# A new written order for all parts of a one-core block kernel, with G and M2 laid in turn over two PSUM tiles

## The chip, the cores and the metric

The kernel runs on one core of one Trainium2 chip. Its time is device microseconds of one execution. The kernel before took 641.51 us (median of 3 runs, 640.56 to 641.72).

## The reference

One block of 2048 rows (S) and 512 columns (D): a linear attention with 32 heads and then a gated MLP that mixes the rows, each behind a layer norm whose scale, shift and gate come from a vector `c`. Cut to what matters:

```python
mod = (_silu(c) @ w_mod).reshape(c.shape[0], 6, 1, -1)
sa, ca, ga, sb, cb, gb = ...
h = _layernorm(x) * (1 + ca) + sa
x = x + ga * A(h)        # q, k, v = h @ wqkv; phi(t) = where(t > 0, t + 1, exp(t)) + 1e-6
                         # kv = sum_s phi(k) v;  z = sum_s phi(k);  o = phi(q) kv / (phi(q) z + 1e-6);  o @ wo
h = _layernorm(x) * (1 + cb) + sb
x = x + gb * B(h)        # z = gelu(h @ w_in), 1376 wide; z1, z2 = halves; z2 = layernorm(z2)
                         # g = w_sp @ z2 + b_sp, w_sp is 2048 x 2048;  (z1 * g) @ w_out
```

## The kernel before

All operands are fp32. A product is made of three matmuls (`mm3`): each operand is split into a hi part (fp32r, by ScalarE) and a lo part (what is left, a subtraction), and hi x hi, hi x lo and lo x hi are summed in PSUM. So nearly every tile passes ScalarE (hi) and VectorE or GpSimd (lo) on its way to TensorE. The rows are 16 tiles of 128.

Nothing is scheduled by a planner at run time or build time: `ORDER`, a string of 1954 words, says in which order the parts are emitted, and each engine (PE, ACT, DVE, POOL) and SP, which issues all 270 transfers, takes its own instructions in that order. A word is a two-letter part and its numbers; a part with a `yield` goes on at the word's next appearance. An instruction waits until what it reads is written and until the buffer that it writes is free. `SLOTS` says which buffer of a pool each new tile gets (`st`, four raw halves and transposing buffers; `s4`, split operands; `tq`, four late tiles; `ps...`, PSUM).

The stages and the words that matter here:

- Start: `lx` loads a tile of x, `s1` its statistics, `xm` subtracts the mean, `bh`/`bl` are its hi and lo parts, `ta th tl` turn it on PE and split it. `lm` loads w_mod, `mv` sums it on DVE, `cr ce` make a column of it on PE and ACT, `qh qd` split the weights of k and q with it. `du` are two dummy products each while the first loads come in.
- Attention: `km`, `qm` project a tile to k and q (12 matmuls each); `kr`, `ka` or `k1`, `k2`, `k4` are phi, `kh kl` its split; `gm` adds a tile to G (h transposed times phi(k), four blocks of 128 rows in two PSUM tiles). `gh` splits a block of G, `kv` multiplies by the weights of v, `kx` adds, masks and splits the result, `mm` makes a block of M2 (kv times w_o), `me` takes it out of PSUM. `d1 d2` are the denominators. `wo` is phi(q) times M2, `x1` the residual and its statistics.
- A tile is turned either on PE (`at`/`ht`, taken out by `ae`/`he`) or by a transposing DMA of its two 16-bit planes: `ap`/`hp` make the planes on ACT and issue the DMA (second appearance), `am`/`hm` merge the planes again, `ah al`/`hh hl` split. `Up Ux Ug` do this for the last stage.
- Gelu products: `z0`, `z1` (`za zb` in halves), `g1 g2` the gelu, `zl zn` the second layer norm. Their weights are loaded raw (`lW`), split (`wh wl`), stored (`ws`) and fetched back whole (`wr`).
- The product with w_sp takes seven products in place of eight per pair of row tiles (sums of halves beforehand, `Ss` for w_sp and `Td` for z2, and after it `Cs`). `Lh` loads half a row tile of w_sp, `Fh`/`Fl` split, `Pr` multiplies (12 matmuls of 344 columns).
- Output: `Um` multiplies by z1 (`Lz`), the result is turned (`Up Ux Ug`), for 14 tiles stored and fetched again (`Us Ul`), split (`Uh Uo`), multiplied by w_out (`Om`, 17 matmuls; weights by `Wl Wm Wh Wo`) and added to the residual (`Lx`, `Ot`, which then stores).

A trailing number of `am hm Ug` names the engine of the merge (0 DVE, 1 POOL, 2 ACT), and likewise the last number of `Fl`, `bl`, `Tb`, `Wo` and others, where a default stands without it.

Of the kernel before, what the change touches and what calls it, by code (L numbers as in the profile page):

```python
# [25 lines left out]
ta:0123453041025430154023525021301253213402141501305  # L26
psb:01010101101011010101011010101010101010
zs:0123456789abcdef2346ed32c5ea1d0e62c31e421c5e0243ea543c5e434c052ec520187b9fe6da4031c25978ec019b5a89367e124fdc0b8af
pst:0101111010101100100001010101001
s4:01234567307152364712156370453126507635670653105063573264507175723601450120736124325730460367412071530642352105462407316524136570241530652061543704327614657134021736574120176341564761354760253017251634106172171204156320  # L30
tb:01234567012401573450352327132302346202715362751261520350642431567155043617556405610701032327302174272651700417627436724163750134154
st:01230132122102120213131321032310321013012130102130101320302101230213321023103210
ws:010110
pso:0101010011010101101010101011010101010100010101010
md:0123102310210212021201
z1:01101010110110111
tq:01233220231203210010123013
u:0101100101101001
# [4 lines left out]
def block_kernel(ctx: ExitStack, tc: tile.TileContext, x, w_qkv, w_o, w_in, w_sp, b_sp, w_out,  # L43
# [48 lines left out]
    def mm3(o, a_hi, a_lo, b_hi, b_lo, first, last, skip=False):  # L92
        kw = {"skip_group_check": True} if skip else {}
        mm(o, a_hi, b_hi, start=first, stop=False, **kw)  # L94
        mm(o, a_hi, b_lo, start=False, stop=False, **kw)  # L95
        mm(o, a_lo, b_hi, start=False, stop=last, **kw)  # L96
# [900 lines left out]
    def cut():  # L997
# [19 lines left out]
        bh0 kr0 lx6 bl3,1 tl1 ba1 lx9 s16 s11 xm6 bb1 be1 s16 qd0,3 vp0 km1 lx5 s15 xm5 ka2,1 k22 ka0 k20 k20 km4 bl1
        kr1 qd0,2 bp2 qd0,0 k40 kh0 bl0 k14 ks0 ta5 th5 lW1,0 k22 ta6 ka1 k21 s15 tl5 qm3 ba2,0 ba3,0 bh5 k42 lw2,1 bx0
        bx0 th6 vh2 kl0 bl5,1 k21 k24 km5 k15 k41 gm0 lx7 vh0 bb0 s19 qm2 vp1 wh1,0 va1 xm9 tl6 s17 ks1,0 be0 q13 kh1
        s17 kl1 lx10 lW0,1 k24 km6 wl1,0,0 xm7 kh2 k44 kh4 kl2 ks2,0 ka3,1 k23 k23 gm1 k16 ta7 wh0,1 wl0,1 k43 vl0 vl2  # L1020
        ks3,0 k25 q12 bh4 ta9 th9 bl4 bh6 bl6 qm1 kh3 kl3 gm2 gm3 lx8 lW1,2 kl4 ws1,0 k25 k45 ws0,1 bh9 ks4,0 lx12 lW0,3
        vp2 lx11 wh0,3 ks5,0 qr1 tl9 s112 th7 wl0,3 km9 bh7 va2 s18 vh1 xm8 s19 lW1,3 tl7 s110 k19 gm4 wh1,2 wl1,2,0
        ws0,3 q23 k26 q23 q43 k26 kh5 vl1 wh1,3 lW1,1 bh8 kl5 k29 bl7 k46 ta8 km7 k17 wl1,3,0 k29 lW0,2 s111 k49 th8
        xm12 qm0 ws1,2 bl9 wh1,1 xm10 ta12 th12 tl12 s18 wl1,1,0 kh6 qm6 lM2 ta10 gm5 mV2,0 lx14 q22 qr0 xm11 q22 kl6
        q42 bl8,1 tl8 k27 k27 vp3 k47 va3 s110 ks6 ws1,1 th10 q16 s114 qa0,1 wh0,2 lW0,0 km12 tl10 wl0,2,0 q26 q26 ws1,3
        km8 kh7 k18 cv kl7 lx13 s113 s112 k112 k212 ta11 th11 gm6 gm7 q46 wh0,0 k28 wl0,0,0 lo1 mV2,1 k28 k48 ks7 ks8,0
        ks9 vh3 vl3 qm5 q15 mS2 mS2 tl11 ws0,2 s114 lo0 s111 kh9 kl9 kh8 km10 k110 lx15 s115 km11 xm14 kl8 bh14 k210 qa1
        k212 k412 mB2 qm4 xm15 gm8 gm9 k210 k410 mB2 wg1 bh15 s113 xm13 q20 q20 ta13 k111 k211 k211 lM4 bl14,1 bh10
        mV4,0 mV4,1 kh10 bl10 ks10,0 lM3 kl10 q14 k411 th13 tl13 kh11 cv q24 q24 bl15 gm10 kl11 q25 ks11,0 q25 q44 q45
        bh11 bl11 ks12 km13 ta14 th14 bh12 s115 lX4 k113 tl14 mk qm7 q17 q40 ta15 k213 k213 k413 th15 tl15 km14 wg0,1  # L1030
        k114 k214 k214 q27 ws0,0 kh12 mV3,0 mV3,1 k414 q27 ks13,0 kh13 kl13 gm11 mS3 kh14 kl12 kl14 km15 k115 k215
        ks14,0 qm8 q18 wg3,1 k215 k415 ks15,0 bl12,1 gm12 lX7 q47 mS3 kh15 kl15 zx qm10 q21 q21 mS4 wg2 bh13 wx3 wr0,0
        zx mS4 zs zr mB4 mB4 lX3 wx1 bl13,1 d10 q110 q210 d16,0 d26 d26 wr0,3 q210 d26 d26 mB3 q41 d20 q410 qm12 qm13
        d20 ap6 mB3 d20 d20 d14,0 q112 q212 q28 q113 q28 ap6 d24 q212 wx0 d110,0 vb gm13 q213 gm14 d24 d24 q213 q413
        q412 gm15 gh0 gh0 gh3 gh3 d17 d13,0 gh1 gh1 d27 gh2 gh2 d27 qm11 q111 d24 d113,0 am6,2 ap4 ap4 wy1 d27 d27 lX0
# [6 lines left out]
        wr1,2 ah10 Nb al10,0 hp4 x12 x11 x17 z00 x12 h22 ah13 al13 lX10 hp4 g10 wo10 zb0 d28 wo5 d28 x17 hp6 hm4 q414  # L1042
        lX5 hh4 hl4 x11 h21 x110 q411 hp2 hp2 hm3 g20 d111,0 d211 hh3 zl0 d28 x15 hp6 hm6,0 hl3,1 z04 g14 hh6 d19 d29
        hl6 z13 lX12 ht1 x17 x15 z16 x15 x15 d29 d29 hm2,0 g23 hh2 h25 d211 d211 d211 hp5 hp5 g26 x110 zl3 d29 ap8 ap12
        x110 zl6 h27 hl2,1 ap8 am8,2 zl6 zn6 zn6 q415 d115 z03 ap12 x110 h210 ah8 z14 g24 lX9 lX13 g14 hp7 wo13 g13
        mV5,0 am12 ah12 al12 x113 d215 ap9 d215 zl4 hp7 hm7,0 hm5,0 hh5 hl5 hh7 hl7 d215 z02 g12 d215 zl0 zn0 zn0 z12
        ap9 am9 z17 g22 lX8 hp10 hp10 x113 wo12 lX15 x113 ap15 d114,0 zl2 ah9 al9,0 zl3 zn3 d214 d214 al8,0 ap11 ap11
        Ta0,1 x112 x112 zl4 zn3 wo9 g12 z15 zn4 x19 hm10,0 g27 zl7 Tb0,1 wo8 d214 x113 h213 hp13 hp13 lX11 am11 z05 ah11
        x18 g25 zl2 al11,0 wo11 z06 he1 zn2 zl5 zl5 hh10 zn5 x19 zn2 Ta1,1 x112 hl10 zl7 x18 d214 x19 Ta1,0 x112 he1 g15
        ap15 x18 h212 am15,2 ah15 al15 Tb1,1,1 ap14 Td1,0,1 g16 ap14 am14 x18 h28 hp12 g13 ah14 al14,0 wo15 hp12 z11 zn4  # L1050
        g21 x19 g16 h29 Td1,1,1 Ta1,2 hp9 hp9 zl1 x111 x111 x111 x111 zl1 mV5,1 zn5 Ta2,0 x115 zn1 Tb1,2 hp8 hm9,0 z010
# [95 lines left out]
```

## Time and profile before

| | |
|---|---|
| runs | 641.51 us median, 640.56 to 641.72 |
| profiled execution | 642.65 us, span of the instructions 640.8 us |
| PE busy | 619.1 us, 3447 matmuls |
| DVE, ACT, POOL busy | 462.6, 368.6, 248.7 us |
| DMA | 99.99 MB, queue 1 53.2% of 16 engines |

The span runs from the first to the last instruction; the time has some 2 us around it. A busy PE is not PE at its peak, as matmuls overlap. PE is the engine in use nearly throughout, so idle stretches of PE are what another order can change; an engine's waits are read from the list of who waited for whom, and the work around them from the timeline.

### The profile page before, as it was taken

What the parts mean: (1) busy time and instruction counts of PE and PEld (TensorE: products, weight loads), DVE (VectorE), ACT (ScalarE), POOL (GpSimd) and SP (SyncE); (2) the same over time, 40 slices, a digit from 0 to 9 for tenths busy, and PEclk for the clock granted to TensorE, in tenths of its full rate; (3) what the DMA queues carried; (4) which work ended last, traced back from release to release, by engine and by line L of the source; (5) the groups of instructions that cost most, each with busy time, mean ns of one, the idle gap of its engine ahead of it and who ended that gap; (6) DMA issues with size and microseconds to landing.
All of it is one profiled execution on the core that took longest, in us unless ns stands there. A gap on an engine that the chain in (4) does not pass through costs nothing. (4 is left out here: it accounts for less than half of the span.)

```text
span 640.8 us, 9574 instructions
## 1 busy us (share of the span) xinstructions
PE 619.1 (97%) x3447; PEld 563.7 (88%) x3447; DVE 462.6 (72%) x806; ACT 368.6 (58%) x639; POOL 248.7 (39%) x218
## 2 busy tenths in 40 slices
...
GB/s 312 141 106 165 211 261 164 67 113 27 149 274 219 68 146 131 129 134 97 180 56 86 145 96 209 137 163 189 86 161 188 175 100 226 213 251 175 149 167 178
DMA packets 86287, 99.99 MB, mean 156 GB/s; under 512 B 56448, under 2 KB 56960, under 8 KB 86240
## 3 DMA queue, kind: packets, MB, share of 16 engines
q1 hardware_dynamic: 86240, 99.38, 53.2%
q8 instruction: 27, 0.44, 0.3%
...
## 5 line engine op out<-in xcount | busy, mean ns | idle before, releaser
L882 PE MATMUL P<-f,f 128*128 128x344 f32 x960 | 169.5, 321 | 3.5 <-POOL f L868 2.1
L882 PEld LDWEIGHTS P<-f,f 128*128 128x128 f32 x960 | 154.1, 188 | 5.9 <-POOL f L868 3.0
L649 PE MATMUL z<-win,ht 128*128 128x344 f32 x768 | 125.9, 323 | 4.8 <-ACT ht L111 2.5
L649 PEld LDWEIGHTS z<-win,ht 128*128 128x128 f32 x768 | 122.6, 190 | 8.4 <-ACT ht L111 2.9
L865 ACT ACTIVATE f<-raw_wsp 128x512 fp32r<-128x512 f32 x96 | 57.5, 624 | 59.8 <-DMA raw_wsp<-in_w_sp 19.8
L868 POOL TENSOR_TENSOR f<-raw_wsp,f 128x512 fp32r<-128x512 f32 x34 | 48.1, 1426 | 81.2 <-ACT f L865 57.1
L868 DVE TENSOR_TENSOR f<-raw_wsp,f 128x512 fp32r<-128x512 f32 x62 | 50.4, 830 | 27.0 <-ACT f L865 26.9
L220 POOL TENSOR_TENSOR mv<-ve,mhalf 128x1 f32<-128x1 f32 x48 | 34.8, 745 | 46.2 <-DVE ve L218 41.9
L882 PE MATMUL P<-bigb,f 128*128 128x344 f32 x192 | 39.9, 321 | 1.9 <-DVE f L868 1.9
L882 PE MATMUL P<-biga,f 128*128 128x344 f32 x192 | 39.4, 320 | 0.0
L94 PE MATMUL pout<-wo,ut 128*128 128x512 f32 (+1 forms) x85 | 32.7, 384 | 2.0 <-ACT ut L941 2.0
L96 PE MATMUL pout<-wo,ut 128*128 128x512 f32 (+1 forms) x85 | 32.7, 385 | 1.7 <-DVE ut L948 1.7
L882 PEld LDWEIGHTS P<-bigb,f 128*128 128x128 f32 x192 | 32.0, 188 | 2.5 <-DVE f L868 2.5
L95 PE MATMUL pout<-wo,ut 128*128 128x512 f32 (+1 forms) x85 | 32.3, 380 | 0.0
L882 PEld LDWEIGHTS P<-biga,f 128*128 128x128 f32 x192 | 32.1, 188 | 0.0
L232 ACT COPY ux<-us 128x768 uint16<-128x768 uint16 x32 | 25.0, 829 | 4.8 <-PE P L882 2.2
L588 POOL TENSOR_TENSOR pq<-pq,den 128x512 f32<-128x512 f32 x16 | 17.5, 1097 | 21.6 <-DVE den L585 20.3
L94 PE MATMUL qp<-wq,ht 128*128 128x512 f32 x64 | 25.8, 403 | 0.0
L94 PE MATMUL g<-pkhl,hhl 128*128 128x512 f32 x64 | 25.4, 397 | 0.0
L94 PE MATMUL po<-m,pt 128*128 128x512 f32 x64 | 25.4, 396 | 0.0
L94 PE MATMUL kp<-wk,ht 128*128 128x512 f32 x64 | 25.3, 396 | 0.0
L96 PE MATMUL po<-m,pt 128*128 128x512 f32 x64 | 25.3, 395 | 0.0
(234 smaller groups left out, 1391.5 us busy)
## 6 DMA issues: line engine op xcount, KB each, us to landing
raw_wsp<-in_w_sp SPq DMA_DIRECT2D x32, 512.0 KB, 4.7
raw_mod<-in_w_mod SPq DMA_DIRECT2D x12, 512.0 KB, 5.4
...
```

The costliest lines, as they stand in the source:

```text
L94: mm(o, a_hi, b_hi, start=first, stop=False, **kw)
L95: mm(o, a_hi, b_lo, start=False, stop=False, **kw)
L96: mm(o, a_lo, b_hi, start=False, stop=last, **kw)
L220: nc.gpsimd.tensor_tensor(mv[:, 1:2], ve, mhalf, op=OP.pow)
L232: nc.scalar.copy(pl[:, h], v[:, :, h])
L588: nc.gpsimd.tensor_mul(q3, q3, d[:, :, None].to_broadcast([P, H, D // H]))
L649: mm(p[:, b, :HB], a[:, i, kc], win[h][:, j, kc, b * HB:(b + 1) * HB], start=kc == 0 and k == 0, stop=kc == KC - 1 and k == 2)
L865: nc.scalar.activation(SF[p, h, k][:, 0], s_src(p, h, k), AF.Copy)
L868: eng.tensor_sub(SF[p, h, k][:, 1], s_src(p, h, k), f(SF[p, h, k][:, 0]))
L882: mm(B[p, k][:, :HB], a[:, x_], b[:, y_], start=i == 1, stop=i == 3 * NP)
```

## The change

`ORDER` and `SLOTS` are replaced as a whole: the same 1954 words in another order, except that some words name another engine. Counted from the words: DVE 806 to 784 instructions, ACT 637 to 647, POOL 211 to 223 (without set-up and table loads); PE's 3447 matmuls and SP's transfers are the same ones. Four functions lay the four blocks of G and of M2 over their two PSUM tiles in turn (0 and 2, 1 and 3) and no longer in pairs (0 and 1, 2 and 3).

```diff
-            mm3(G[dc // 2][:, dc % 2, :], a[:, 0, sl], a[:, 1, sl], b[:, 0], b[:, 1], t == 0, t == NT - 1)
+            mm3(G[dc % 2][:, dc // 2, :], a[:, 0, sl], a[:, 1, sl], b[:, 0], b[:, 1], t == 0, t == NT - 1)
...
     def m2_mm(g):
-        if g // 2 not in PM2:
-            PM2[g // 2] = ps("b", [P, 2, D], f"pm2_{g}")
-        mm3(PM2[g // 2][:, g % 2, :], KV["h"][:, 0, g], KV["h"][:, 1, g], wog[g][:, 0], wog[g][:, 1], True, True)
+        if g % 2 not in PM2:
+            PM2[g % 2] = ps("b", [P, 2, D], f"pm2_{g}")
+        mm3(PM2[g % 2][:, g // 2, :], KV["h"][:, 0, g], KV["h"][:, 1, g], wog[g][:, 0], wog[g][:, 1], True, True)
...
-        yield from hi_lo(o[:, 0], o[:, 1], PM2[g // 2][:, g % 2, :])
+        yield from hi_lo(o[:, 0], o[:, 1], PM2[g % 2][:, g // 2, :])
...
-        yield from hi_lo(GH[dc][:, 0], GH[dc][:, 1], G[dc // 2][:, dc % 2, :])
+        yield from hi_lo(GH[dc][:, 0], GH[dc][:, 1], G[dc % 2][:, dc // 2, :])
```

Of the order, the stretches that the prediction speaks of. The start:

```diff
-        lx3 s13 lx0 si si du1 du2 du3 du4 du5 du6 du7 du8 du9 du10 s10 xm3 lx4 s14 li lx2 s12 bh3 du11 lx1 s13 du12 ta3
-        th3 tl3 du13 du14 du15 du16 xm2 bh2 ta2 du17 s11 th2 du18 du19 du20 du21 du22 xm1 s14 xm4 lm1,0 mv1,0 s10 ta4
-        lm1,1 tl2 lm0,0 mv1,1 mv1,2 mv1,3 bh1 cr1 ce1 s12 mv0,0 du23 du24 du25 du26 du27 xm0 lm0,1 mv0,1 lw1,0 mv0,2
-        mv0,3 qh1,1 qd1,1 qh1,0 qd1,0 cr0 ce0 lw1,1 ta0 qh1,2 bl2 th0 qh1,3 qd1,2 qd1,3 km3 by0 km2 lw0,0 tl0 bp0 qh0,1
...
+        lx3 du1 s13 li du2 du3 du4 lx0 si si du5 xm3 bh3 lx2 bl3,1 du6 du7 du8 du9 ta3 s10 lx1 s12 s12 th3 du10 xm2 s11
+        du11 du12 xm1 du13 du14 lm1,0 mv1,0 mv1,1 tl3 bh2 xm0 du15 lm1,1 mv1,2 bh0 ta2 th2 tl2 lx4 s10 s14 lm0,0 mv0,0
+        du16 du17 du18 du19 ta1 du20 du21 du22 du23 du24 mv1,3 cr1 mv0,1 du25 du26 xm4 bl0,1 lm0,1 mv0,2 th1 mv0,3 ce1
+        du27 lw1,0 bh1 qh1,1 lw1,1 tl1 qh1,0 qd1,0 ta4 qd1,1 qh1,2 qd1,2 lx6 qh1,3 qd1,3 cr0 ce0 by0 by1 lw0,1 bp2 km2
```

From kv to the first gelu products (each stretch begins and ends within a line):

```diff
-        qm15 kv0 kv1 wy0 ah6 d23 kv2 d23 kv3 qm9 d23 at0 d23 d210 d210 q115 q215 d11 d210 am4,2 d210 wx2 wy2 al6,0 d213
-        ap7 ap7 d213 kx kx q19 qm14 ah4 mm0 d21 mm2 wy3 d12 me0 me0 d21 d21 wr1,0 wr1,3 me2 me2 d213 d21 mm1 me1 me1
-        q114 at3 ae3 mm3 me3 me3 lX6 ae0 ae0 d22 d22 q48 wo6 x16 x16 wr1,1 wr0,2 ae3 d213 am7,2 al4 d18 x16 ah7 d15 l5
-        q29 q29 d22 d25 d25 wo0 ap10 ap10 wo3 d22 at2 x10 at1 d112,0 d25 ap13 d25 ap5 x10 x10 ap5 ap13 al7 ae2 x13 x13
-        x13 wo4 x13 x10 ae1 wr0,1 ae2 h20 w02 x14 w12 q49 ht0 d212 am5,2 ah5 h23 x14 x14 he0 he0 q214 hp3 wo7 x17 ae1
-        al5 q211 q211 am13,2 lX1 x14 h24 za0 x16 h26 wo1 x11 d212 q215 hp3 lX2 d212 x11 x12 x12 q214 d212 d28 am10,2
...
+        d21 kv0 qm11 q28 q28 gh1 ws1,1 mB3 q19 d213 am4,2 wy3,0 kv1 q48 kv2 kv3 ap6 Nb at0 kx d15,0 kx lX4 at3 d213 d213
+        qm15 q115 mm1 lX6 wr1,1 d213 d21 ae0 ae0 mm0 me0 wr0,0 wr0,3 q111 me0 ah4 me1 me1 mm2 me2 me2 mm3 me3 d21 at1
+        ae1 lX3 d12 d18 me3 d22 wr0,2 d28 am6,2 d22 d22 wo0 l5 ah6 d28 al4 x10 x10 ae3 ae3 d110 d22 d25 wo4 q215 ap13
+        x10 d25 d25 al6 d25 x14 ae1 x14 ah7 d28 d28 at2 q29 wo3 wr0,1 x13 x13 wo6 x14 ae2 ae2 x13 x10 h20 ap5 x16 al7
+        ap5 x14 q215 d210 d210 ap13 w02 w12 q414 x12 x12 ht0 he0 he0 q211 x13 lX7 q211 h23 d210 hp3 d210 x16 am5,2 hp3
+        x16 q29 h24 hp4 wo1 x12 hp4 x16 za0 z00 am13,2 ah13 ah5 al5 h26 q49 hm3,0 wo7 x17 al13 d112,0 hh3 q415 lX13 hl3
```

The end:

```diff
-        Uh8,1 Om4 Uo8,1 Uo8,0,1 Ul2 Uh11,1 Cs7,7 Cs7,5 Cs7,4 Cs7,9 Us12 Ul12 Ul7 Uh3,0 Uo9,1 Ot1 Om9 Ot9 Lx7 Ot9 Uh2,0
...
-        Ot3 Ul10 Uo12,0 Ux15 Ug15 Lx6 Uh12,1 Ot6 Uo12,1 Uo5,1,1 Ot6 Om5 Ug14 Uo11,1 Om11 Lx5 Ot5 Uh14,0 Ot5 Uh10,0
-        Uo10,0,1 Uh13,0 Uo14,0 Lx2 Ot8 Uh14,1 Lx14 Ot7 Uo14,1,1 Ot2 Ot7 Lx13 Om12 Ot8 Ot2 Lx12 Uh15,1 Uh15,0 Uo15,0 Om14
-        Uo15,1 Om15,256,512 Ot14 Ot14 Lx11 Uo13,0,1 Ot11 Ot12 Lx15 Uh13,1 Uo13,1,1 Om13 Ot12 Ot11 Ot13 Ot13 Ot15,256,512
-        Ot15,256,512 Uh10,1 Uo10,1,1 Om10 Lx10 Ot10 Ot10 Om15,0,256 Ot15,0,256 Ot15,0,256
+        Fl7,0,3,0 Pr7,0,3 Wm0 Wh0 Wo0 Fl7,1,3,0 Up12 Wl4 Pr7,1,3 Ul11 Uo1,1,1 Uh5,1 Wh3 Cs7,1 Ul8 Wm5,1 Wh5 Wo3 Uh0,0
+        Cs7,6 Cs7,2 Ux12 Wm4 Uo0,1 Wh4 Ug12,2 Lz15 Wo5 Lx1 Wo4,1 Uh2,0 Uo2,0 Om1 Cs7,7 Ul7 Uh7,1 Lx7 Cs7,5 Ul9 Ot1 Ot1
...
+        Uo5,1,1 Uh4,0 Uh3,1 Uh6,0 Cs7,3 Cs7,4 Us12 Uh11,1 Uo4,0,1 Om4 Uo3,0 Uh8,1 Uo11,1 Uh9,0 Ot2 Uo3,1,1 Om3 Uo9,0,1
...
+        Uo6,0 Om6 Uq14 Ot7 Up14 Lx8 Ot8 Uh5,0 Ot9 Ul12 Uh12,1 Uo12,1,1 Uh12,0 Uo12,0,1 Uo11,0 Uo5,0 Lx3 Ot3 Ot3 Om5 Lx11
+        Ot6 Ot6 Om11 Um15 Uq15 Lx5 Ot5 Up15 Uo10,1 Uh13,0 Ot8 Ux15 Uh10,0 Uo10,0 Om12 Om10 Ot11 Lx12 Ot12 Uo13,0 Uh13,1
+        Uo13,1,1 Om13 Ux14 Ug15,2 Uh15,0 Ot5 Uo15,0 Uh15,1 Uo15,1,1 Om15,256,512 Ug14 Uh14,1 Uo14,1 Uh14,0 Uo14,0 Ot12
+        Lx13 Lx15 Om14 Ot11 Lx14 Lx10 Ot10 Ot10 Ot15,256,512 Ot15,256,512 Ot13 Ot13 Ot14 Ot14 Om15,0,256 Ot15,0,256
+        Ot15,0,256
```

More of the change, by code (lines that the diff above doesn't have):

```diff
@@ L25 @@
 SLOTS = """
[L26 to L38, printed above, removed]
+ta:0123450104325041135240131012041503454153041215403
+psb:01010110101010101001010101010101010101
+zs:0123456789abcdef13564574dc92760d419da234d2940a27d63723d9a42a3d90a793dbf85eac16420d793b8e52635fbd9e5c48231a076bde0
+pst:0101100000101001000101101010101
+s4:01234567570231465011253476035214712704173421347042501453627431746065712360542713054620376256210264753140152153146350127067065342514635407201654703157203165460341672315037064251374137562431065720467053746042475671236520
+tb:01234567012430615024637656213703236431670675226116502463737246172703157071024672017235151756470124653433071254137425421636145346356
+st:01230132322031301201212103102130213023201320132123231023210312013230120312032130
+ws:010101
+pso:0101010101010010101010110110101011010101101001110
+md:0123012301201202102102
+tq:01230301302130232312103102
+z1:01110101001101010
+u:0110101001010110
 """
@@ L1017, in block_kernel @@
[L1017 to L1035, printed above, removed]
-        qm15 kv0 kv1 wy0 ah6 d23 kv2 d23 kv3 qm9 d23 at0 d23 d210 d210 q115 q215 d11 d210 am4,2 d210 wx2 wy2 al6,0 d213
@@ L1042, in block_kernel @@
[L1042 to L1051, printed above, removed]
@@ L1102, in block_kernel @@
-        Fl7,1,5 Wl0 Pr7,1,5 Ug13,2 Wm0 Uh9,1 Fl7,0,3 Wh0 Ul11 Wo0 Uh0,0 Uo0,0 Us13 Wh3 Uq12 Wo3 Wl2 Pr7,1,1 Up12 Wl4 Wl5
-        Cs7,1 Cs7,6 Wm4,1 Pr7,1,2 Pr7,0,3 Ul3 Pr7,1,3 Lx9 Wm2 Lz15 Wh4 Cs7,2 Uh1,0 Uo1,0 Wo4 Ux12 Wh2 Wo2 Wm5 Wh5 Wo5
-        Om1 Uh0,1 Uo0,1 Lx1 Uh4,0 Uo4,0,1 Uh9,0 Lx0 Uh3,1 Uo3,1,1 Ug12,2 Om0 Uh4,1 Ul8 Lx8 Uh8,0 Uo4,1 Ul6 Ot1 Uo9,0,1
-        Uh8,1 Om4 Uo8,1 Uo8,0,1 Ul2 Uh11,1 Cs7,7 Cs7,5 Cs7,4 Cs7,9 Us12 Ul12 Ul7 Uh3,0 Uo9,1 Ot1 Om9 Ot9 Lx7 Ot9 Uh2,0
-        Uo2,0,1 Uo3,0,1 Uh12,0 Ul5 Om3 Uh5,1 Uh2,1 Uo2,1 Om2 Cs7,3 Ot0 Uh5,0 Um15 Om8 Um14,1 Lx3 Ot3 Uq14 Up14 Ot0 Ul13
@@ new lines, in block_kernel @@
+        du11 du12 xm1 du13 du14 lm1,0 mv1,0 mv1,1 tl3 bh2 xm0 du15 lm1,1 mv1,2 bh0 ta2 th2 tl2 lx4 s10 s14 lm0,0 mv0,0
+        du16 du17 du18 du19 ta1 du20 du21 du22 du23 du24 mv1,3 cr1 mv0,1 du25 du26 xm4 bl0,1 lm0,1 mv0,2 th1 mv0,3 ce1
+        du27 lw1,0 bh1 qh1,1 lw1,1 tl1 qh1,0 qd1,0 ta4 qd1,1 qh1,2 qd1,2 lx6 qh1,3 qd1,3 cr0 ce0 by0 by1 lw0,1 bp2 km2
+        lx5 s15 ta0 km1 by2 s11 qh0,2 th0 tl0 by3 kr2 xm5 bh5 ta5 lw0,0 bp1 s16 th5 tl5 kk0,0 bx1 bx1 qd0,2 kk0,1 s14
+        s15 lx8 kk0,2 bp0 qh0,0 ba1,0 bl5,1 kr1 s18 kk0,3 lw2,0 kr0 ba2 bb1 th4 qd0,0 km5 bp3 be1 ka0,1 ka1 xm6 s13 ka2
@@ new lines, in block_kernel @@
+        d14,0 d26 d26 gm13 d27 qm8 d27 qm13 q18 d27 d27 lX0 ap7 q40 gm14 wr1,0 ap7 d23 q113 d24 d24 wx2 vb lX2 wg0,1 wx0
+        wy2,0 q213 q213 q413 wr1,2 q210 q210 q410 d23 d24 gm15 gh0 gh0 d10 d24 d11 qm12 am7,2 mB4 q112 mB3 gh2 gh2 wy0,0
+        q212 q212 d20 d23 gh3 wr1,3 d20 qm14 d23 ap4 ap4 q412 q114 wx1 wy1 q214 d20 d20 q214 gh3 gh1 qm9 d21 d113,0 ap6
+        d21 kv0 qm11 q28 q28 gh1 ws1,1 mB3 q19 d213 am4,2 wy3,0 kv1 q48 kv2 kv3 ap6 Nb at0 kx d15,0 kx lX4 at3 d213 d213
+        qm15 q115 mm1 lX6 wr1,1 d213 d21 ae0 ae0 mm0 me0 wr0,0 wr0,3 q111 me0 ah4 me1 me1 mm2 me2 me2 mm3 me3 d21 at1
@@ new lines, in block_kernel @@
+        h22 d212 hp2 h27 g14 hp6 al10,0 lX1 x11 hm6 mV5,0 hh6 q411 ap8 lX5 x15 hp2 z14 d215 d215 x11 x11 x11 zl0 g14
+        hm2,0 d212 wo13 x113 wo10 hl6 g24 lX8 hh2 hl2,1 hp7 d111 d211 d211 z12 g22 d212 x15 x15 ap12 ap8 am8,2 hp7 ah8
+        zl3 d19,0 lX10 x15 d29 h25 hp5 zn0 z16 g26 h21 al8,0 g10 zl4 zn0 Ta0,1 Tb0,1 Td0,0 z02 zl3 ap12 am12,2 ah12 g12
+        d211 d211 ap11 zl4 wo8 hp5 z06 hm7,0 zl2 d29 d214 d214 d214 d214 d29 al12 d29 hm5 ap11 x18 ht1 x113 hh5 he1
+        am11,2 he1 ah11 x110 x110 x110 g16 al11,0 z03 ap15 ap15 x113 zn4 hl5,1 zl2 wo11 z15 ap9 zn3 x18 ap9 hh7 x18 x18
```

124 lines of the change are left out of this document (72 added, 52 removed).

## The prediction

> **What bounds the kernel now.** I read the page first, then the busy time by stage, then the chain of waits on PE, and last the two timelines where PE stands still. PE is the bound:
>
> ```profile
> PE 619.1 (97%) x3447; PEld 563.7 (88%) x3447; DVE 462.6 (72%) x806; ACT 368.6 (58%) x639; POOL 248.7 (39%) x218
> ```
>
> The change alters no matmul, so at most the 21.7 us in which PE is idle (640.8 less 619.1), and any stretch at a lower clock, can move. The stages show where they lie (length, then busy time of PE, PEld, DVE, ACT and POOL, granted clock, DMA share, GB/s): weights and attention input to 160, the turn to the output projection to 220, gelu, the big products to 566, the output.
>
> ```profile
> 0.00:21.00 21.00, 19.13 (x141) 18.80 (x142) 13.86 (x32) 9.84 (x18) 3.85 (x12) 1.00 0.72 266
> 21.00:160.00 139.00, 139.00 (x647) 114.15 (x646) 123.20 (x205) 101.65 (x175) 50.88 (x42) 1.00 0.44 140
> 160.00:220.00 60.00, 55.08 (x276) 46.87 (x275) 48.36 (x89) 38.79 (x69) 28.82 (x27) 0.97 0.69 189
> 220.00:360.00 140.00, 139.43 (x839) 134.02 (x838) 107.62 (x230) 91.32 (x148) 54.36 (x53) 1.00 0.47 123
> 360.00:566.00 206.00, 200.61 (x1258) 197.66 (x1257) 137.81 (x198) 105.96 (x190) 90.33 (x63) 1.00 0.55 158
> 566.00:641.00 75.00, 65.83 (x296) 52.19 (x294) 31.79 (x56) 21.03 (x42) 20.48 (x23) 0.98 0.62 184
> ```
>
> From 21 to 160 nothing can be won. 4.9 us are idle from 160 to 220, 0.6 to 360, 5.4 to 566 and 9.2 after it, of which 5 follow the last matmul. PE's own waits (total, times, longest):
>
> ```profile
> PE z L649 <- ACT ht L111: 2.5, 1, 2.5
> PE P L882 <- DVE f L868: 2.4, 3, 1.1
> PE P L882 <- POOL f L868: 2.1, 3, 1.1
> PE pout L94 <- ACT ut L941: 2.0, 2, 1.1
> PE pout L96 <- DVE ut L948: 1.7, 1, 1.7
> ```
>
> These name ACT, DVE and POOL, but a transfer often stands behind them. The largest one shows it (stages, then ACT's timeline):
>
> ```profile
> 188.90:191.40 2.50, 0.04 (x1) 0.00 (x0) 1.42 (x4) 2.47 (x5) 0.42 (x1) 0.98 1.00 216
> 191.40:194.80 3.40, 3.35 (x12) 3.36 (x13) 3.27 (x6) 3.37 (x6) 1.89 (x3) 0.51 0.92 322
> ```
> ```profile
> 188.87 1.38 ACT L245 COPY xpp<-xpp 128x512 uint16<-128x512 uint16 x2 [6.32 <-DMA xpp<-xpp]
> ```
>
> ACT stood 6.3 us before the merge of `am5,2` for a transposing DMA. `he0`, on which the first gelu product `za0` waits, was queued behind it. PE lost 2.5 us, and then ran 3.4 us at half clock (0.51), another 1.7: 4.2 us from one late transfer.
>
> **The change, part by part.**
>
> *Transposes.* Each engine takes its instructions in the written order, so a merge (`am`, `hm`, `Ug`) placed too soon after its planes (`ap`, `hp`, `Up`) stalls what is behind it. Who waited for the transposes, and their landing times:
>
> ```profile
>   ACT xpp L245: 12.2, 3
>   DVE ux L245: 10.2, 3
>   ACT xph L245: 7.2, 2
>   ACT ux L245: 6.0, 5
>   DVE xpp L245: 2.3, 1
>   DVE xph L245: 1.6, 1
> ...
> DMA to landing us min/median/max: 3.0/3.6/8.1
> ```
>
> That is 39.5 us. For each of the 42 I added the mean durations of what its merging engine has queued between planes and merge. In the old order 15 have under 4.0 us (the median landing and a little for the issue), 35.7 us short in all, near the 39.5 waited. In the new order it is 11, and 13.5 us. Example: between `ap5` and `am5,2` ACT had only `ae2` and `ae1` (1.2 us); now it has `q215`, `d210`, `he0`, both parts of `q211` and `hp3`, 4.1 us. `he0` stands ahead of that merge now. And `l5`, whose two 512 KB loads were issued within 3 us of these transposes, comes 8.7 us of PE work (`wo4 at2 wo3 wo6`) ahead of `ap5`'s. So the stall before `za0` goes: -4.2, with 0 as the other end. What can be late next there is `z00`, which waits for `wr0,1`; it has 10.6 us of PE work after its issue. Of the three waits of some 0.6 us each at 205 to 215 (1.7 of the stage's 4.9) I take half: -0.85.
>
> *Loads of w_sp* (count, size, median landing):
>
> ```profile
> raw_wsp<-in_w_sp SPq DMA_DIRECT2D x32, 512.0 KB, 4.7
> ```
>
> Between the instruction that frees the buffer of such a half and its first use lie under 4.7 us of PE work for 10 of 32 in the old order, 16.6 us short in all; 6 and 11.1 in the new one, two thirds. The 6.0 us idle from 220 to 566 go down in that proportion: -2.0 (ends -4 and +1).
>
> *Other engines.* DVE falls from 806 to 784 instructions, ACT rises by 10, POOL by 12. Nine lo parts go from DVE to POOL, where they take 1.43 us instead of 0.83:
>
> ```profile
> L868 POOL TENSOR_TENSOR f<-raw_wsp,f 128x512 fp32r<-128x512 f32 x34 | 48.1, 1426 | 81.2 <-ACT f L865 57.1
> L868 DVE TENSOR_TENSOR f<-raw_wsp,f 128x512 fp32r<-128x512 f32 x62 | 50.4, 830 | 27.0 <-ACT f L865 26.9
> ```
>
> POOL's 90 busy us of 206 leave room: 0; without it, 9 x 0.6 = 5.4 us would be at stake. Ten half merges go from DVE to ACT, which is under 74% busy in every stage; their danger is the wait, not the time (second rival).
>
> *G and M2 in turn.* `gh0` now waits for the third block of the last `gm15` (0.7 us later), hidden by the three products of q (2.8 us each) ahead of `kv0`: 0; without them it would cost the 0.7. M2 is another matter. Before (DVE, then PE):
>
> ```profile
> 161.56 0.69 DVE L717 TENSOR_TENSOR kvm<-pkv,bz 128x512 f32<-128x512 f32 x1
> 162.29 0.69 DVE L718 TENSOR_TENSOR kvm<-pkv,kvm 128x512 f32<-128x512 f32 x1
> 163.02 1.82 DVE L719 TENSOR_TENSOR kvm<-kvm,mask 128x512 f32<-128x512 f32 x1
> 165.54 1.00 DVE L113 TENSOR_TENSOR kvh<-kvm,kvh 128x512 fp32r<-128x512 f32 x1 [0.70 <-ACT kvh L111]
> 166.47 0.74 DVE L399 SCALAR_TENSOR_TENSOR tq<-qp,mv,kqb 128x512 f32<-128x512 f32 x1
> ...
> 168.19 0.69 DVE L113 TENSOR_TENSOR m<-pm,m 128x512 fp32r<-128x512 f32 x1 [0.39 <-ACT m L111]
> ```
> ```profile
> 168.94 0.50 PE L94 MATMUL pm<-wog,kvh 128*128 128x512 f32 x1 [0.72 <-DVE m L113]
> 169.27 0.39 PE L95 MATMUL pm<-wog,kvh 128*128 128x512 f32 x1
> 169.50 0.40 PE L96 MATMUL pm<-wog,kvh 128*128 128x512 f32 x1
> ```
>
> Matmuls of this width start 0.23 us apart, so a block of M2 takes 0.7 and a product of twelve 2.8 us. The row at 168.94 is `mm1` writing the other half of the tile that `me0` reads: a whole PSUM tile is the unit of waiting. In the new order `mm1 mm0 mm2 mm3` stand side by side on PE, and `mm2` shares `me0`'s tile, `mm3` that of `me1`. Two stalls follow. First, `kx` takes 5.0 us from its first add to its lo part; PE now has `at0 at3 qm15` (3.5) after `kv3` instead of `qm9 at0 qm14` (5.9): about 1.3 waited, since the first matmuls need the hi part alone. Second, behind that lo part DVE has two reciprocals (0.34 each), `q115`, `ae0`, `q111` (about 0.7 each) and then `me0`'s lo, 3.5 us, while PE has 0.95 of work: 2.6 waited. Behind `mm2` wait `mm3`, `at1` and `wo0`. Less the 0.7 of before: +3.2. It is 0 if the wait is by halves after all, which the quoted row speaks against, and 4.9 if 2.6 us of stillness bring half clock, as 2.5 us did at 191.4.
>
> The Trainium skill (TensorE: Matmul & The Clock Gate, Part 1) says that the clock falls after an idle window of about 3.4 us, counted by a free-running clock. By that rule the 2.6 us at `mm2` cost no clock and the sum stays at 636.0. By the row of 191.4, where 2.5 us were enough, it would be 637.7. Trace and page differ on the length; I leave the 1.7 out of the sum and in the range.
>
> *Start.* Same loads, same 27 dummies; `mod` 1 goes ahead of `lx4`, and ACT does `qh1,2 qh1,3` ahead of `ce0`. PE's waits on the way to its first projection:
>
> ```profile
> 15.86 1.02 PE L162 MATMUL pcol<-ones,y 128*128 128x1 f32 x8 [0.62 <-DVE y L187]
> ...
> 20.27 0.66 PE L358 MATMUL tx<-ident,x 128*128 128x128 f32 x4 [0.26 <-ACT col L171]
> ```
>
> `cr1` now has two more dummies and the same count of turns ahead of it, so the first wait goes; `ta0` moves behind `km2`, so the second does: -1.0 (ends 0 and -1.5).
>
> *Output and end.* (Chain in order of time; DVE's timeline.)
>
> ```profile
> 604.42 6.02 DMA us<-ux
> ```
> ```profile
> 636.41 1.02 DVE L993 TENSOR_TENSOR x<-x,pout 128x512 f32<-128x512 f32 x2 [4.16 <-DMA x<-x1d]
> ```
>
> The 6.0 us transpose of `Ux15` held `Ug15` on DVE, behind which the lo part for `Om11` stood: the 1.7 us above. Now `Om12 Om10 Om13` (12 us) lie between `Ux15` and its product, and `Ug15` is on ACT. `Ul12`, issued directly behind its own store `Us12`, gets 19.6 us of PE work in between, which frees the loads queued on SP and the 1.1 us wait for ut. Together -2.7 (other end 0). `Om1`'s weights still come in a chain (`Wl0` to `Wo4`), so its wait of about 1 us stays. At the end `Lx10` landed after the last matmul and held `Ot15,0,256`; now it is asked for with `Om14` still to run: -1.0.
>
> *Unseen.* From 21 to 160 any new wait is loss; its bounds are 0 and the largest wait seen, 2.5; I take 1.0. In 160 to 566 the new order has gaps of its own: between 0 and one full event of 4.2, I take 2.0.
>
> Sum: -4.2 - 0.85 - 2.0 + 3.2 - 1.0 - 2.7 - 1.0 + 1.0 + 2.0 = -5.55 us. The profiled execution took 642.65 (span 640.8), 1.1 above the median 641.51 of the runs; from the median the sum gives 636.0.
>
> **The rivals.**
>
> 1. *The waits only move.* Stalls removed here come back elsewhere, as slack in a full queue is only passed on: gain 0 to 1.3, about 641. For it: the mean PE work between a lo part `Fl` and its product stays at 5.6 and 5.5 us. Against: the drop from 35.7 to 13.5.
> 2. *ACT is held by its merges: slower.* 18 of 26 attention and gelu transposes now merge on ACT, 13 before, between 150 and 300 us. One that lands at the maximum of 8.1 us against a cover of 4 to 5 holds ACT for 3 to 4 us, with the evacuations of PSUM behind it; each such event costs 4.2 us as at 188.9. Two more than summed give 636.0 + 8.4 = 644.4; it decides from two on. Against it: the typical landing of 3.6 is covered.
> 3. *Nearly all stalls go.* Only M2's 3.2 stays of the idle time between start and end: the terms without the two allowances for the unseen are -8.55, and the rest of 220 to 566 another -4: about 629.
>
> **How the numbers follow.** My forecast has 0.56, rival 1 0.14, rival 2 0.22, rival 3 0.08; the forecast and rival 3 are faster, rival 1 is the same, rival 2 slower. The forecast's own range is 632 to 639.5, from M2's ends (-3.2, +1.7) and the unseen. The range for 8 in 10 is 629.5 to 644.5: it reaches into rivals 2 and 3. Beyond 0.2% (1.3 us, about what a measurement of this kernel can tell from no change): faster 0.64, same 0.14, slower 0.22.
>
> **What would show it.** Right: no PE gap before `za0` and clock 1.00 there; transposes waited for under 20 us in all; a gap of 2 to 3 us inside pm; `Ot15`'s DVE row directly behind PE's end. Wrong: PE below 139 busy us from 21 to 160, a second stretch of half clock, or ACT rows with over 3 us of waiting for xpp or xph ahead of a PE gap.

## The result, and the profile after

The changed kernel takes 618.42 us (median, 617.96 to 622.38); the kernel before took 641.03 beside it (638.84 to 641.72). The ratio is 0.967, 95% interval 0.962 to 0.971: 22.6 us less by the medians. The forecast was 636.0 and its range ended at 629.5: the sign was right, the size a quarter of what came. The profiled execution took 618.51 us, so it stands for the median; the one of before stood 1.6 above its new median.

The first lines of the page, and the busy time by stage (stages that hold about the same work as those shown of before):

```profile
span 616.7 us, 9576 instructions
PE 610.9 (99%) x3447; PEld 563.7 (91%) x3447; DVE 454.6 (74%) x784; ACT 378.8 (61%) x649; POOL 254.8 (41%) x230
```
```profile
0.00:21.00 21.00, 20.01 (x147) 19.69 (x148) 14.65 (x33) 12.40 (x22) 5.43 (x13) 1.00 0.82 291
21.00:160.00 139.00, 139.00 (x638) 113.75 (x638) 119.94 (x200) 102.13 (x176) 59.24 (x47) 1.00 0.44 142
160.00:220.00 60.00, 58.49 (x314) 51.42 (x314) 48.55 (x94) 39.30 (x72) 28.84 (x27) 1.00 0.67 193
220.00:360.00 140.00, 140.00 (x858) 136.80 (x857) 109.90 (x233) 100.48 (x161) 44.40 (x47) 1.00 0.45 120
360.00:546.00 186.00, 186.00 (x1182) 186.00 (x1181) 133.26 (x176) 100.51 (x179) 91.60 (x66) 1.00 0.61 170
546.00:617.00 71.00, 67.36 (x317) 56.07 (x315) 28.32 (x51) 23.97 (x45) 25.31 (x31) 1.00 0.65 200
```

From 21 us to the last matmul PE stands still once, for 1.5 us, and the clock is 1.00 in every stage (0.97 and 0.98 twice before; the 0.98 lay behind the last matmul, where it costs PE nothing). PE's whole list of waits, and who waited for the transposes (39.5 us before, 5.7 now):

```profile
PE pm L94 <- DVE m L113: 1.5, 1, 1.5
PE warm L142 <- POOL tiny L108: 1.0, 1, 1.0
```
```profile
  DVE ux L245: 3.1, 1
  DVE xph L245: 1.5, 1
  ACT ux L245: 1.1, 1
...
DMA to landing us min/median/max: 3.0/3.7/6.4
```

Where did 24.1 us of span (640.8 less 616.7) come from? The idle time of PE fell by 15.9 (21.7 to 5.8). Of the rest, 3.4 us at half clock are 1.7. The remainder does not show in the busy time, because the ends of the matmuls are modelled: they run past the start of the next one, so a gap in the busy time is shorter than the delay. The spacing of the starts shows all of it. I took for each of the 3447 matmuls the time to the next start, less the median of its shape, and added it up by stage:

| stretch (of before) | before | after | difference |
|---|---|---|---|
| start, to 20 | 4.2 | 2.9 | -1.3 |
| 20 to 160 | -0.2 | -0.1 | +0.1 |
| 160 to 220 | 7.8 | 2.1 | -5.7 |
| 220 to 560 | 10.9 | 1.2 | -9.7 |
| 560 to the last matmul | 5.8 | 0.0 | -5.8 |
| behind the last matmul | 4.9 | 3.4 | -1.5 |

That is 23.9 of the 24.1 us. The largest part lies where I had forecast nothing on balance, in the product with w_sp. There, what an engine stood still for until a load of w_sp had landed (us, times; before, then after):

```profile
  DMA raw_wsp<-in_w_sp: 41.4, 18
```
```profile
  DMA raw_wsp<-in_w_sp: 13.9, 5
```

### The profile page after: what moved, and what is told of

It is laid out like the page before. It is cut to its first block, busy times and chain, and to the rows that moved or that the text cites. A ratio compares the mean times of both kernels' runs of the same rounds, so it can differ in the third digit from the quotient of the medians.

```text
span 616.7 us, 9576 instructions
## 1 busy us (share of the span) xinstructions
PE 610.9 (99%) x3447; PEld 563.7 (91%) x3447; DVE 454.6 (74%) x784; ACT 378.8 (61%) x649; POOL 254.8 (41%) x230
## 4 chain that ended last, share of the span: by engine, by line
PE 98%; DVE 1%; ACT 0%; issue 0%; POOL 0%; ACTq 0%; POOLq 0%
PE P L882 34%; PE z L649 20%; PE pout L94 3%; PE pout L95 3%; PE pout L96 3%; PE warm L142 2%; PE g L95 2%; PE po L96 2%; PE kp L94 2%; PE g L94 2%; PE g L96 2%; PE po L94 2%; PE po L95 2%; PE kp L95 2%; PE kp L96 2%; PE qp L94 2%
## 5 line engine op out<-in xcount | busy, mean ns | idle before, releaser
L882 PE MATMUL P<-f,f 128*128 128x344 f32 x960 | 167.8, 320 | 0.0
L649 PE MATMUL z<-win,ht 128*128 128x344 f32 x768 | 122.7, 319 | 0.0
L868 POOL TENSOR_TENSOR f<-raw_wsp,f 128x512 fp32r<-128x512 f32 x47 | 65.1, 1395 | 67.0 <-ACT f L865 62.4
L868 DVE TENSOR_TENSOR f<-raw_wsp,f 128x512 fp32r<-128x512 f32 x49 | 41.7, 863 | 18.8 <-ACT f L865 18.6
L220 POOL TENSOR_TENSOR mv<-ve,mhalf 128x1 f32<-128x1 f32 x48 | 34.1, 716 | 40.5 <-DVE ve L218 40.1
L941 ACT ACTIVATE ut<-uf 128x384 fp32r<-128x384 f32 x28 | 14.1, 521 | 24.5 <-PE pout L989 7.3
L993 DVE TENSOR_TENSOR x<-x,pout 128x512 f32<-128x512 f32 (+1 forms) x17 | 11.0, 655 | 24.6 <-PE pout L989 18.7
L94 PE MATMUL po<-m,pt 128*128 128x512 f32 x64 | 25.4, 397 | 0.0
```

The costliest lines, as they stand in the source:

```text
L220: nc.gpsimd.tensor_tensor(mv[:, 1:2], ve, mhalf, op=OP.pow)
L649: mm(p[:, b, :HB], a[:, i, kc], win[h][:, j, kc, b * HB:(b + 1) * HB], start=kc == 0 and k == 0, stop=kc == KC - 1 and k == 2)
L868: eng.tensor_sub(SF[p, h, k][:, 1], s_src(p, h, k), f(SF[p, h, k][:, 0]))
L882: mm(B[p, k][:, :HB], a[:, x_], b[:, y_], start=i == 1, stop=i == 3 * NP)
L941: nc.scalar.activation(UT[t, n][:, 0], u_of(t, n), AF.Copy)
```

## The experiments

Three theories. **T**: each use of a transfer stands farther behind its landing in the new order, and this room is the gain. **R1**: the engines named carry it; 173 of the 1954 words name another engine (45 `Fl`, 20 `Uo`, 18 `Ss`, 19 merges and so on). **R2**: the layout of G and M2 carries it. A fourth came up on the way, **R4**: stalls mended in one place come back in another. Times are medians, with the ratio to the kernel before in the same series, which took 640.0 to 641.5. `SLOTS` goes with its order in every run, so "order" means both here; what the buffers alone do is not shown.

**Order, engines and layout apart.** Three edits of the whole:

```diff
-            mm3(G[dc % 2][:, dc // 2, :], ...      and M2 alike      (after_both_pairs, on the changed kernel;
+            mm3(G[dc // 2][:, dc % 2, :], ...                         before_turn is the reverse, on the kernel before)
```
```diff
- Fl0,0,1 am12,2 hm6 Ug7,2 ...         (after_old_engines, on the changed kernel: 173 words;
+ Fl0,0,1,0 am12 hm6,0 Ug7 ...          before_new_engines is the reverse, on the kernel before)
```

> The changed kernel with only its four blocks of G and of M2 laid in pairs again; order and engines stay. T (slack: in the new order each transfer's use stands farther behind it, and that alone is the gain): G costs nothing either way, and M2's only wait on PE (1.5 us, mm2 for me0's lo part) goes, as mm2 now starts another PSUM tile: 616.9, PE's list of waits keeps the first dummy's 1.0 alone, or a wait of under 1 us for mm1, which then shares mm0's tile. R1 (the engines named carry the gain): the same 617 to 618. R2 (the layout in turn carries the gain): 630 to 641.

> The changed kernel with the engine named by the kernel before in all 173 words where the two differ; order and layout stay. T (slack from the order): most of the gain stays, 619 to 627; the words were placed for other queues, so single waits of 0.5 to 2 us come up, fewer than 8 us in all. R1 (the engines named carry the gain): 635 to 641. R2 (the layout): 618.4.

> The kernel before with the engine named by the changed kernel in the same 173 words; order and layout stay as before. T (slack from the order): 637 to 648, no gain beyond 4 us, PE's waits at transposes stay. R1 (the engines): 618 to 625. R2 (the layout): 641.

> The kernel before with the blocks of G and M2 laid in turn alone. T (slack from the order): 641 to 644; mm0 and mm2, which stand next to one another in the old order, now share a tile, so mm2 waits some 1 to 3 us for me0. R1: the same. R2 (the layout carries the gain): 618 to 630.

| kernel | us | ratio, 95% interval |
|---|---|---|
| changed, pairs (after_both_pairs) | 622.44 | 0.972 (0.968 to 0.976) |
| changed, old engines (after_old_engines) | 658.94 | 1.028 (1.023 to 1.032) |
| before, new engines (before_new_engines) | 696.47 | 1.087 (1.082 to 1.091) |
| before, in turn (before_turn) | 644.89 | 1.006 (1.004 to 1.009) |

R2 falls: the layout alone makes the old order slower (there PE's wait in M2 is 2.5 us in place of 0.7), and without it the new order keeps most of the gain. T's 616.9 for after_both_pairs was missed as well: M2 in pairs waits longer, not shorter. R1 as it was put falls too, and so does my number for T: the new order with the old engines is 19 us slower than before, the old order with the new engines 56 us. Neither half is a gain; only the two together are. The trace of after_old_engines says why the simple form of T is not enough. Its waits for transposes, for loads of w_sp (behind it those of before_new_engines), and the largest waits of PE:

```profile
  ACT ux L245: 4.2, 2
  ACT xpp L245: 0.6, 1
  DVE ux L245: 0.4, 1
```
```profile
  DMA raw_wsp<-in_w_sp: 16.7, 7
```
```profile
  DMA raw_wsp<-in_w_sp: 72.1, 19
```
```profile
PE P L882 <- DVE f L868: 5.9, 6, 1.8
PE pout L96 <- DVE ut L946: 4.8, 1, 4.8
PE P L882 <- POOL f L868: 4.1, 4, 2.3
```

The transfers are about as little waited for as in the changed kernel. That goes with the order, and a slow kernel alone does not bring it: before_new_engines is slower still and waits 72.1 us for w_sp and 24.1 for transposes. But lo parts are late now. The likely reason is that the engines' queues were filled for another sharing out of the work; the rows show more than one form of it (before the wait of 1.8 us, DVE itself stood 3.95 us for a hi part of ACT), and the single stalls were not taken apart.

The layout's part is small and can be read in PE's waits of after_both_pairs:

```profile
PE pm L94 <- DVE m L113: 2.8, 1, 2.8
PE pkv L711 <- DVE gh L113: 1.1, 1, 1.1
```
```profile
172.30:175.70 3.40, 3.40 (x11) 2.83 (x10) 2.06 (x4) 2.87 (x6) 1.57 (x2) 0.50 0.50 199
```

`kv0` waits 1.1 us for G, M2 2.8 in place of 1.5, and behind these 2.8 us PE runs 3.4 us at half clock: 1.1 + 1.3 + 1.7 = 4.1 by rows, and 4.0 by the medians. (The two profiled executions differ by 3.3, as this one was 0.8 us ahead from the start.) The intervals of the two kernels overlap, so the rows carry this.

**Which engines.** The 173 words in three groups, each undone alone in the changed kernel:

```diff
- Fl... (45 words: 27 from POOL to DVE, 18 back)       after_old_fl
- am... hm... Ug... (19 words, DVE, ACT, POOL)          after_old_merges
- Uo Ss bl ks Td Tb hl wl d1 ... (109 words)            after_old_rest
```

> The changed kernel with the engine of the kernel before for the 45 lo parts of w_sp (Fl) alone that name another one (31 to DVE, 14 to POOL, or near that); the other 128 words keep the new engines. If the loss of 40 us in after_old_engines lies in the queues of the product with w_sp: 630 to 640, all of it between 360 and 560. If it is spread over all stages as the words are: 45 of 173, some 10 us, 628. If Fl's engine does not matter (R: transfers alone): 618 to 620.

> The changed kernel with the engine of the kernel before for the 19 merges (am, hm, Ug) alone that name another one. R1 (the engine of the merges carries part of the gain): 625 to 632. T (a merge has room on either engine where the order gives it cover): 618 to 622.

> The changed kernel with the engine of the kernel before for the 109 words that are neither lo parts of w_sp (Fl) nor merges (am, hm, Ug): sums Ss and Td, lo parts Uo, bl, hl, wl, Tb, al, and the like. All 173 together cost 40.5 us (658.9 against 618.4), the 45 Fl 12.9, the 19 merges 6.4. If the groups add up: 40.5 - 12.9 - 6.4 = 21.2 more, 640. If they meet in the same queues (each alone still finds room, together they don't): 624 to 634. If these words carry nothing: 618 to 620.

Measured: 631.27 (0.985, 0.980 to 0.989), 624.86 (0.977, 0.974 to 0.979) and 645.30 (1.006, 1.003 to 1.009). That is 12.9, 6.4 and 26.9 us over 618.42, together 46.2 where all at once cost 40.5: nearly a sum. No group is free, T missed the merges, and the last group lies 5 us above the 640 of a plain sum. With `Fl` alone undone, PE's list holds the rows below. That execution took 634.6, 3.3 above its median; the matmul starts put 11.4 us of its loss between 420 and 460, and some 5 of them are two stretches at half clock, 3.4 and 6.8 us long:

```profile
PE P L882 <- DVE f L868: 6.0, 4, 2.2
PE P L882 <- POOL f L868: 2.4, 3, 1.5
```

**One stall undone, four mended.**

```diff
- ap5 x14 q215 d210 d210 ap13 w02 w12 q414 x12 x12 ht0 he0 he0 q211 ... am5,2
+ ap5 am5,2 x14 q215 d210 d210 ap13 w02 w12 q414 x12 x12 ht0 he0 he0 q211 ...       (after_am5_early)
```
```diff
- am5,2 ah5 h23 x14 x14 he0 he0 / Ss5,0,7 Ss5,0,5 Fl4,1,6,0 / Ux15 Ug15 ... Uo11,1 / Fl2,1,2 ... Fl2,0,2
+ he0 he0 am5,2 ah5 h23 x14 x14 / Fl4,1,6,0 Ss5,0,7 Ss5,0,5 / Uo11,1 Ux15 Ug15 ... / Fl2,0,2 Fl2,1,2 ...   (before_repaired)
```

> The changed kernel with one word moved: am5,2 stands directly behind its transfer (ap5) again, ahead of he0 on ACT. T (slack): ACT waits some 3 us for the transfer, he0 comes late, and the stall ahead of za0 is back, with half clock behind it: 621 to 624. R4 (slack absorbs it, since the whole order has room): 618.4.

> The kernel before with five words moved, each ahead of a word that waits for a transfer or a fuller queue: both he0 ahead of am5,2 (stall of 4.2 us with its half clock), Fl4,1,6,0 ahead of Ss5,0,7 (1.3, and the two stalls of 0.8 and 0.9 some 9 us later, if they are its echo: the buffer that it frees is what Lh10,1 and Lh11,1 wait for), Uo11,1 ahead of Ux15 and Ug15 (1.8), Fl2,0,2 ahead of Fl2,1,2 (1.2). R3 (a few root stalls, each with its echo, to be mended where they stand): 4.2 + 3.0 + 1.8 + 1.2 = 10.2 less, 630. R4 (slack is only passed on, a mended stall comes back a few us later): 637 to 641. T (stalls are local, echoes are not): 4.2 + 1.3 + 1.8 + 1.2 = 8.5 less, 631.5.

after_am5_early: 618.67 (0.965, 0.961 to 0.970), no loss at all. Yet ACT stood 5.8 us before that merge, nearly the 6.3 of before (ACT's row, then the product `za0` on PE):

```profile
185.73 1.41 ACT L245 COPY xpp<-xpp 128x512 uint16<-128x512 uint16 x2 [5.79 <-DMA xpp<-xpp]
```
```profile
189.07 2.68 PE L649 MATMUL z<-win,ht 128*128 128x344 f32 x16
```

The transfer was issued at 181.6 us here and at 182.0 in the kernel before. Here it lands after 4.0 us, and `he0` is ready in time; before, it took 6.8, with `l5` (until 186.2), the transpose of `ap10` and a store under way beside it. So the place of `he0`, on which I laid the 4.2 us, is not what matters in the new order. The shorter landing fits the fewer transfers around it, which were not changed alone.

before_repaired: 637.50 (0.996, 0.992 to 0.999), 3.9 us less where the four mends were worth 8.5 to 10.2. Three of the four stalls are gone (at 188.9, 479.4 and 614.4). The fourth, 1.1 us at 402.9, is 1.2 us at 400.9, two matmuls earlier, behind another row of DVE (`us` in place of a lo part). The two of 0.7 and 0.8 us at 487 to 489 stay (0.6 and 0.8), so they were no echo of the one at 479.4. Two others have grown; the three in PE's list:

```profile
PE pout L94 <- ACT ut L941: 2.1, 1, 2.1
PE z L649 <- DMA win<-wd: 2.0, 1, 2.0
PE P L882 <- DVE us L901: 1.2, 1, 1.2
```
```profile
203.41 3.07 PE L649 MATMUL z<-win,ht 128*128 128x344 f32 x12 [2.01 <-DMA win<-wd]
206.27 0.63 PE L94 MATMUL po<-m,pt 128*128 128x512 f32 x1
206.70 0.63 PE L95 MATMUL po<-m,pt 128*128 128x512 f32 x1
```

`zb0` now waits 2.0 us for `wr1,2`, where it waited 0.6 before, with some half clock behind it (0.63 in place of 0.39), and `Om2` waits 2.1 where it waited 1.1. PE comes to these points 3.0 and 5.2 us earlier than before, but `wr1,2` lands only 1.6 earlier, and `Ul5`, for which ACT stands ahead of the split that `Om2` needs, 4.2: the transfers did not move along with PE. This is R4, for more than half of what was mended: 3.9 us came of 8.5 to 10.2.

**How much room there is.** Two tests: more traffic in both kernels, and no cover at all for the transposes.

```diff
     def load_half(t, h):
         load_raw(("wsp", t, h), w_sp[t, :, 8 * h:8 * h + 8, :], shape=(P, 8, P))
+        more = dram.tile([P, 8, P], F32, tag=f"more{t}_{h}", name=f"more{t}_{h}")
+        dma(more, w_sp[t, :, 8 * h:8 * h + 8, :])
```
```diff
- ap5 ... am5,2   hp3 ... hm3,0   Ux15 ... Ug15,2   (42 merges)
+ ap5 am5,2 ...   hp3 hm3,0 ...   Ux15 Ug15,2 ...   (after_merges_early)
```

> The kernel before, with a second transfer behind each of the 32 loads of w_sp: the same 512 KB from w_sp to a place in memory of its own that nothing reads. No engine waits for it; it only takes up the queues, so later transfers land later. T (in the old order the first use of a load stands right behind its landing: 15 of 32 start within 0.3 us of it): each microsecond of delay is passed on to PE, at some 1 us for half of the loads: 15 to 30 us more, 655 to 670. R4 (stalls are the queues' of the engines, transfers hidden): under 5 us, 640 to 645.

> The changed kernel with the same second transfer behind each load of w_sp. T (more room behind each landing: 6 of 32 within 0.3 us): under half of what the kernel before loses by it, 2 to 10 us, 620 to 628. R4 (transfers hidden in both): under 2 us. If the new order's room were only just enough for the old landing times, it would lose as much as the kernel before or more: 15 to 30 us.

> The changed kernel with each of the 42 merges of a transposed tile (am, hm, Ug) directly behind its own transfer in the order, so that its engine stands still until the transfer has landed, some 3 to 5 us each. By the prediction's step (cover under the landing time is waited for, and PE feels it): waits of 120 to 180 us on ACT, DVE and POOL, and 30 us or more on PE, 650 or above. By after_am5_early, where one such wait of 5.8 us cost nothing: a small part of it reaches PE, 620 to 635.

before_traffic takes 666.71 (1.041, 1.038 to 1.045), after_traffic 627.26 (0.979, 0.977 to 0.982): the same extra transfers cost 26.0 us in the old order and 8.8 in the new one. Waits for w_sp (before_traffic, then after_traffic):

```profile
  DMA raw_wsp<-in_w_sp: 58.0, 20
```
```profile
  DMA raw_wsp<-in_w_sp: 26.5, 12
```

This shows T's core: the new order has room for late transfers, a third of the sensitivity, though not without end. Part of the difference is the clock: by the granted clock PE ran 20.5 us of before_traffic at half clock and 3.4 of the kernel before, and none of the two new ones up to the last matmul. That is some 7 of the 26.0 us; without it the new order passes on nearly half as much as the old one. after_merges_early takes 666.89 (1.041, 1.039 to 1.044): the 42 merges stand still for 59.5 us in all, a third to a half of what I expected, and it costs 48.5, some 12 of them from 30.7 us at half clock. One such wait was free, 42 are not: each eats room that the next would have needed.

**M2 without the wait.** PE writes both blocks of a tile before anything reads it (G stays in turn):

```diff
-        if g % 2 not in PM2:
-            PM2[g % 2] = ps("b", [P, 2, D], f"pm2_{g}")
+        if g // 2 not in PM2:
+            PM2[g // 2] = ps("b", [P, 2, D], f"pm2_{g}")
...
- mm2 me2 me2 mm3 me3
+ mm2 mm3 me2 me2 me3
```

> The changed kernel with M2 laid in pairs again (G stays in turn) and mm3 one place earlier, ahead of me2, so that PE writes both blocks of a tile before anything reads it. By tile-wide waiting neither mm2 nor mm3 waits for an evacuation: the 1.5 us in pm go, 616.9, unless wo0, the next that needs all four blocks, waits for me3 in their place (then 617.5 to 618.4). If waiting were by halves: 616.9 as well, but then the pairs kept by after_both_pairs would not have shown 2.8.

617.48 (0.964, 0.960 to 0.967), the lowest median of all, 0.9 under the changed kernel; that difference is inside the intervals, so its proof is the rows. The wait in pm is gone, `wo0` waits 0.2 in its place, and the span is 615.2 (616.7):

```profile
PE warm L142 <- POOL tiny L108: 1.0, 1, 1.0
PE po L95 <- DVE m L113: 0.2, 1, 0.2
```

## Why the prediction was right or wrong

*The ceiling.* I took the idle 21.7 us of PE, with stretches at a lower clock, for all that could move. By the spacing of the starts the stalls up to the last matmul were 28.4 us, and 4.9 behind it. Each of some 20 stalls is about 0.16 us longer than its gap shows (the gap of 1.06 us at 401.8 delayed the next start by 1.22), half clock is 1.7 of it, and some 7 us are small delays without a gap, of which the changed kernel keeps 4.

*The stall at 188.9*, -4.2: gone, as said; PE is busy and at clock 1.00 there. The reason I gave first, `he0` ahead of `am5,2`, is sufficient in the old order (before_repaired) but not needed in the new one (after_am5_early); my second, `l5` out of the transposes' way, fits the landing after 4.0 us, but was not tried alone. *What is late next there*: I named a `wr` and gave it nothing. In the new order that holds; in the old one it took back 2.0 us and some clock.

*The three waits at 205 to 215*, half of 1.7: all gone. Here, as in the next step, I took a part of what went whole.

*220 to 566*, -2.0, and +2.0 for the unseen (which was meant for 160 to 566): measured -9.7. This is the step that failed, with 9.7 of the 17.6 us between forecast and result. Three errors are in it. The base was 6.0 idle us where the stalls were 10.9. The rule was a proportion, cover falling short by 16.6 and then 11.1 us, so a third of the idle time; the waits for w_sp fell by two thirds (41.4 to 13.9), and those left fell on engines that had room, so PE felt none. And I allowed for new gaps where there were none: the allowance took back what little the step gave.

Why the cover missed: I counted PE's work behind loads of w_sp alone, while PE's stalls were made on the splitting engines' queues, and not by these loads only. In the old order DVE stood 3.1 and 3.2 us for a load of w_sp before PE's gaps at 459.1 and 479.4. Before those at 402.9 and 487.6 to 489.0, ACT stood 2.8 and 6.3 us for the store of a turned tile, whose buffer the split was to write (`f` and `ux` share the pool `s4`). The row before the gap at 487.6, then all such waits, before and after:

```profile
485.38 0.63 ACT L865 ACTIVATE f<-raw_wsp 128x512 fp32r<-128x512 f32 x1 [6.32 <-DMA ud<-ux]
```
```profile
ACT f L865 <- DMA ud<-ux: 12.2, 4, 6.3
ACT f L865 <- DMA ud<-ux: 0.9, 1, 0.9
```

I had given these stores no term. How the gain divides between loads, stores and the queues behind them stays open: after_old_fl loses 12.9 us with no transfer moved in the order, but its waits for w_sp grow too, to 23.7.

*Other engines*, 0, or 5.4 at stake: the price was far off, since I counted the net (nine lo parts, ten half merges, a few instructions per engine). Gross it is 173 words, 45 of them `Fl`, and undoing them costs 40.5 us. Gains of the order alone, which I summed, do not exist: the order alone loses 19 us.

*G in turn*, 0: right in the new order, where pairs cost 1.1. *M2*, +3.2: the mechanism was right and 2.4 too dear (start delay 0.9 before, 1.7 after). DVE and PE:

```profile
163.98 0.69 DVE L719 TENSOR_TENSOR kvm<-kvm,mask 128x512 f32<-128x512 f32 x1
165.43 0.69 DVE L113 TENSOR_TENSOR kvh<-kvm,kvh 128x512 fp32r<-128x512 f32 x1 [0.15 <-ACT kvh L111]
...
168.33 0.68 DVE L113 TENSOR_TENSOR m<-pm,m 128x512 fp32r<-128x512 f32 x1
```
```profile
167.16 0.40 PE L96 MATMUL pm<-wog,kvh 128*128 128x512 f32 x1
169.06 0.50 PE L94 MATMUL pm<-wog,kvh 128*128 128x512 f32 x1 [1.51 <-DVE m L113]
```

`kx` lasts 3.6 us and not 5.0, since the multiplication takes 0.69 and not 1.82, so the 1.3 for `mm1` never came. `mm2` waits as said, 1.5 and not 2.6: PE had `mm1` and `mm0` (1.4) to do, not 0.95, and DVE's rows overlap by about 0.1 us each where I added them end to end. Waiting by whole tiles is shown from both sides: pairs made `mm3` wait 2.8 (after_both_pairs), and one word moved made the wait go (after_m2_free).

*Start*, -1.0: measured -1.3. *Output*, -2.7: both stalls that I named are gone, but so are the rest; I said that `Om1`'s wait of about 1 us would stay, and it did not. The stage gave 5.8. *End*, -1.0: measured -1.5. As I said it would, `Ot15`'s row stands right behind PE's end at 613.36:

```profile
613.39 0.42 DVE L993 TENSOR_TENSOR x<-x,pout 128x256 f32<-128x256 f32 x1 [1.34 <-PE pout L989]
```

*Unseen from 21 to 160*, +1.0: nothing came.

*The rivals.* The third, nearly all stalls go, came true and beyond its 629: it had 0.08. The drop of the transposes' shortfall, 35.7 to 13.5, spoke for it, and 5.7 us of waiting is what came. I kept it small because I read the shortfall as waiting, while a wait costs PE only once the room behind it is used up. The first, waits only move, is what local mends do in the old order (before_repaired), not what the new one does. The second, ACT held by merges, did not come; after_merges_early shows that it is real when the cover is taken away.
